# Weight conversion in 4 KB pieces that also lie in w2's own tile, with three, then five ticks a slot

## The chip, the cores and the metric

The kernel runs on one core of one Trainium2 chip. The metric is the device time of one execution in microseconds (us). Three timed runs of the kernel before gave 1628.86, 1624.64 and 1628.58 us; the median is 1628.58 us.

## The reference

Eight batches of threshold attention (8 heads, 576 positions, 64 features a head) feed a block of layer norm and two matrix products:

```python
scores = scale * np.matmul(q, k.transpose(0, 1, 3, 2))
thresh = np.max(scores, axis=-1, keepdims=True) - tau
scores = np.where(scores >= thresh, scores, -1000000000.0)
attn = np.exp(scores - np.max(scores, axis=-1, keepdims=True))
attn = attn / (np.sum(attn, axis=-1, keepdims=True) + 1e-09)
x = (attn @ v, heads side by side)            # (8, 576, 512)
xn = (x - mu) / np.sqrt(var + 1e-06) * g_ln
out = x + np.maximum(xn @ w_ch1, 0.0) @ w_ch2  # 512 -> 2048 -> 512
```

The two weight matrices arrive as 64-bit floats. [...]

## The kernel before, in words

**Slots.** The attention of one batch is cut into nine slots (s = 0 to 8), 72 slots in all (n = 0 to 71). One slot is: score products on TensorE (`scores`, L324, or L100 for s = 4), row maxima on VectorE (L337), exponentials on ScalarE (L348), threshold and row sums on VectorE (`weights`, L354, then the reciprocal L358), and four multiplications by that reciprocal. Then the weights are transposed: in batch 0 on TensorE (L384, L397, with copies on ScalarE), from batch 1 on by VectorE (L415, L421) and a round trip through DRAM (L427 out, L436 and L437 back). One slot later they are multiplied by v (L460) and the result is copied to x (L477, on ScalarE). Scores and values share PSUM, so the next slot's scores wait for this copy.

**Feed-forward.** Every 288 tokens form a group. A group needs 64 products with w1 (xc to hidden) and 64 with w2 (hidden to p), each two matmuls by `product` (L100). They fill TensorE's idle time inside the slots: `second_part` issues as many steps in each of four quarters of a slot as keep the group on schedule, about 29 a slot. A step whose weights are not yet converted, by the plan's own count, is not issued (`yield 0`, L545, L572); TensorE catches up in later slots.

**Conversion.** The weights are 32 chunks of 128x512 numbers, 16 of w1 and 16 of w2. The class `Weights` moves them along by ticks, at most one of each per tick: `begin` (two operations on VectorE, L211 and L215, two on ScalarE, L219 and L220), `carry` (an integer addition on GpSimd, L226) and, three ticks later, `end` (a selection on VectorE, L231; for w1 a multiplication by g on ScalarE, L236, which writes w1). `fetch` issues the DMA of a chunk's 512 KB (L199). A chunk in work occupies one place of 8 KB per partition: 4 KB of raw words, 2 KB for `a`, 2 KB for `y`. There are five such places: two in `stage`, two in `hidden` (until chunk 10), one in `et`'s buffer (until chunk 24). A place is given back by `end`, which issues the next fetch into it at once. Ticks are at points 0 and 2 of slots 0 to 3, at 0, 2 and 3 of slots 4 and 5, and at 0 to 3 from slot 6 on (L649).

**Order.** Every engine runs its instructions in the order in which this Python code writes them; nothing is reordered. SyncE (SP) issues nearly all DMAs in one queue, and an instruction that waits there holds back all behind it.

Of the kernel before, what the change touches and what calls it, by code (L numbers as in the profile page):

```python
# [18 lines left out]
def kernel(  # L19
# [66 lines left out]
    w2_sb = [consts.tile([128, DM], F32, name=f"w2_{i}") for i in range(ND)]  # L86
# [73 lines left out]
    class Weights:  # L160
# [12 lines left out]
        def __init__(self):  # L173
            self.chunks = [
                (w1_sb[i][:, c : c + WC], w_ch1[i * 128 : (i + 1) * 128, c : c + WC], i)
                for c in range(0, DF, WC)
                for i in range(NK)
            ] + [(w2_sb[i], w_ch2[i * 128 : (i + 1) * 128, :], None) for i in range(ND)]
            self.n1 = NK * (DF // WC)
            self.fetched = self.begun = self.carried = self.ended = 0  # L180
            self.at, self.due, self.ticks = {}, [], 0
            flat = hidden.rearrange("p d t -> p (d t)")
            stage = consts.tile([128, 2 * 4 * WC], F32, name="stage")
            et0 = att.tile([128, NB, 128], F32, tag="et", bufs=1, name="et0")
            own = [stage[:, i * 4 * WC : (i + 1) * 4 * WC] for i in range(2)]
# [15 lines left out]
        def parts(self, i):
            at = self.at[i][0]
            raw = at[:, : 2 * WC]
            both = lambda t: raw.bitcast(t).rearrange("p (n two) -> p n two", two=2)
            return both, at[:, 2 * WC : 3 * WC], at[:, 3 * WC :]

        def begin(self):
            both, a, y = self.parts(self.begun)
            self.begun += 1
            au, hi = a.bitcast(U32), both(U32)[:, :, 1]  # L210
# [8 lines left out]
            nc.scalar.activation(both(I32)[:, :, 0], both(U32)[:, :, 0], func=AF.Copy, scale=2.0**-29)  # L219
            nc.scalar.activation(y, both(F32)[:, :, 1], func=AF.Square)  # L220

        def carry(self):
            both, a, y = self.parts(self.carried)
            self.carried += 1
            ai = a.bitcast(I32)
            nc.gpsimd.tensor_tensor(out=ai, in0=ai, in1=both(I32)[:, :, 0], op=ALU.add)  # L226

        def end(self):
            both, a, y = self.parts(self.ended)
            dst, _, gi = self.chunks[self.ended]  # L230
# [403 lines left out]
    if w_ch1.dtype == I64:  # L634
        conversion.fetch()
    else:
# [10 lines left out]
    for n in range(NS):  # L647
        b, s = divmod(n, SLOTS)
        ticks = ((0, 2) if n < 4 else (0, 2, 3) if n < 6 else (0, 1, 2, 3))  # L649
# [10 lines left out]
        run(n, 0)  # L660
        run_all(stores)
# [10 lines left out]
        weights(b, es, thr)  # L672
# [64 lines left out]
```

## Time and profile before

| | |
|---|---|
| median of three runs | 1628.58 us |
| profiled execution, its own time | 1629.46 us |
| its span in the trace | 1627.6 us |
| TensorE busy | 1438.3 us, 88% |
| VectorE busy | 832.7 us, 51% |
| ScalarE busy | 463.3 us, 28% |
| GpSimd busy | 456.1 us, 28% |
| granted TensorE clock, mean | 0.957 |

Busy shares are means over the whole span. The span has two parts: about 400 us in which weights are converted and the first groups run, and a regular part in which every nine slots look alike. A share of the span says little about the first part, so it is read slot by slot. A slot is taken to begin with its first row maximum (L337).

### The profile page before, as it was taken

The numbers are of one execution on the slowest core, as the hardware profiler recorded it, in microseconds if no ns is written. First come the engines' busy times: TensorE is split into PE (matmuls) and PEld (weight loads), VectorE is DVE, ScalarE is ACT, GpSimd is POOL, SyncE is SP. The second block draws the span as 40 slices with busy tenths as digits, with TensorE's granted clock in tenths as the row PEclk, the third lists the DMA queues.
The fourth block names the chain that finished last, engine by engine and source line by source line (L and its number), as shares of the span: only waits on it lengthen the run. The fifth ranks groups of instructions, "written<-read, shape, count | busy, mean of one in ns | idle before, by whom it ended". The sixth has DMA issues, their size and how long they took to land.

```text
span 1627.6 us, 28865 instructions
## 1 busy us (share of the span) xinstructions
PE 1438.3 (88%) x11700; PEld 851.4 (52%) x11700; DVE 832.7 (51%) x1380; ACT 463.3 (28%) x831; POOL 456.1 (28%) x703
## 2 busy tenths in 40 slices
PE   3658834899989999999999999899999999999998
PEld 2434412565555655555555655565555655555554
DVE  6767655324455554655555554645555554645210
ACT  4666522122313231232313131322223131323120
POOL 3444332212222222323232332323132322323100
PEclk9778957999999999999999999999999999999999
DMA  8322345533567455755566446655566547645400
GB/s 160 98 69 82 78 114 136 142 85 79 120 151 175 125 141 124 162 150 141 133 149 171 128 128 146 151 152 128 146 143 164 128 128 165 149 122 138 111 11 15
DMA packets 460694, 205.08 MB, mean 126 GB/s; under 512 B 275024, under 2 KB 420176, under 8 KB 460560
## 3 DMA queue, kind: packets, MB, share of 16 engines
q1 hardware_dynamic: 458160, 202.93, 51.0%
q8 instruction: 92, 1.51, 0.4%
q10 hardware_dynamic: 2368, 0.30, 0.1%
q14 instruction: 42, 0.34, 0.1%
q0 software_dynamic: 32, 0.00, 0.0%
HBM read 119.41 MB, written 83.76 MB: 125 GB/s over the span
## 4 chain that ended last, share of the span: by engine, by line
PE 60%; SPq 10%; DVE 10%; issue 6%; ACT 5%; DMA 5%; POOL 3%; POOLq 0%; DVEq 0%; ACTq 0%
PE p L100 42%; PE sc L460 8%; PE sc L324 7%; SPq L112 7%; DVE e L354 3%; DMA em<-scr 3%; DVE neg L337 2%; ACT e L348 2%; SPq L427 2%; POOL e L363 2%; PE sc L100 2%; DVE et L421 1%; ACT hidden L554 1%; PE tp L384 1%; DMA stage<-in_moe_w_ch_dram 1%
## 5 line engine op out<-in xcount | busy, mean ns | idle before, releaser
L100 PE MATMUL p<-hidden,w 128*64 128x288 f32 x4096 | 518.4, 409 | 46.6 <-DVE w L231 46.6
L100 PE MATMUL p<-xc,w 128*64 128x288 f32 x4096 | 523.4, 411 | 30.9 <-ACT hidden L554 25.5
L100 PEld LDWEIGHTS p<-hidden,w 128*64 128x64 f32 x4096 | 298.1, 138 | 240.9 <-DVE w L231 49.3
L100 PEld LDWEIGHTS p<-xc,w 128*64 128x64 f32 x4096 | 293.5, 138 | 240.5 <-ACT hidden L554 45.3
L337 DVE TENSOR_REDUCE neg<-sc 128x2 f32<-128x1152 f32 x144 | 189.6, 1353 | 347.2 <-PE sc L324 269.8
L363 POOL TENSOR_SCALAR e<-e,den 128x576 f32<-128x576 f32 x270 | 207.4, 785 | 359.7 <-DVE den L358 330.2
L348 ACT ACTIVATE e<-sc,neg 128x576 f32<-128x576 f32 x288 | 194.1, 743 | 269.6 <-DVE neg L337 269.4
L354 DVE SCALAR_TENSOR_TENSOR e<-sc,thr,e 128x576 f32<-128x576 f32 x288 | 220.0, 813 | 37.1 <-ACT e L348 36.4
L324 PE MATMUL sc<-kT,qT 64*128 64x512 f32 (+3 forms) x1024 | 159.8, 452 | 36.4 <-DVE e L354 10.8
L421 DVE STREAM_TRANSPOSE et<-e 128x1152 f32<-128x1152 f32 x112 | 152.8, 1371 | 67.8 <-POOL e L363 60.4
L460 PE MATMUL sc<-em,v_in 128*64 128x256 f32 (+1 forms) x1536 | 158.3, 353 | 26.4 <-DMA em<-scr 17.9
L554 ACT ACTIVATE hidden<-p 128x288 f32<-128x288 f32 x256 | 103.2, 413 | 267.5 <-PE p L100 267.4
L324 PEld LDWEIGHTS sc<-kT,qT 64*128 64x128 f32 x1024 | 88.9, 197 | 122.7 <-issue 78.0
L341 POOL TENSOR_SCALAR thr<-neg,low_sb 128x2 f32<-128x2 f32 x144 | 38.9, 270 | 373.5 <-DVE neg L337 373.5
L460 PEld LDWEIGHTS sc<-em,v_in 128*64 128x64 f32 x1536 | 102.8, 147 | 77.1 <-issue 28.7
L477 ACT COPY x<-sc 128x256 f32<-128x256 f32 x64 | 23.7, 371 | 361.7 <-PE sc L460 346.0
L518 DVE TENSOR_TENSOR o<-p,rb 128x288 f32<-128x288 f32 x64 | 28.1, 439 | 124.9 <-PE p L100 124.9
L519 POOL TENSOR_TENSOR o<-o,x 128x288 f32<-128x288 f32 x64 | 50.9, 796 | 111.7 <-DVE o L518 111.2
L486 POOL TENSOR_TENSOR sum<-sum,x 128x256 f32<-128x256 f32 (+1 forms) x64 | 32.7, 511 | 143.8 <-ACT x L477 141.2
L269 DVE STREAM_TRANSPOSE kT<-k_in 128x576 f32<-128x576 f32 x32 | 24.8, 775 | 90.2 <-DMA k_in<-in_k_dram 86.3
L460 PE MATMUL sc<-rest,v_rest 128*64 128x256 f32 (+1 forms) x384 | 50.9, 340 | 0.0
L566 DVE RECIPROCAL rb<-rb 128x288 f32<-128x288 f32 x16 | 31.3, 1954 | 37.8 <-ACT rb L565 37.8
(71 smaller groups left out, 684.4 us busy)
## 6 DMA issues: line engine op xcount, KB each, us to landing
scr<-et SPq DMA_DIRECT2D x252, 288.0 KB, 4.9
em<-scr SPq DMA_DIRECT2D x63, 1024.0 KB, 5.9
stage<-in_moe_w_ch_dram SPq DMA_DIRECT2D x22, 512.0 KB, 3.9
q_in<-in_q_dram SPq DMA_DIRECT2D x128, 72.0 KB, 3.3
out_dram<-ot SPq DMA_DIRECT2D x256, 36.0 KB, 4.2
k_in<-in_k_dram SPq DMA_DIRECT2D x124, 72.0 KB, 2.6
v_in<-in_v_dram SPq DMA_DIRECT2D x64, 128.0 KB, 2.6
rest<-scr SPq DMA_DIRECT2D x63, 128.0 KB, 5.9
```

The costliest lines, as they stand in the source:

```text
L100: nc.tensor.matmul(out[r], lhsT=lhsT[:, r], rhs=rhs, **flags)
L112: (engines[i] if engines else nc.sync).dma_start(out=t[32 * g : 32 * g + 32], in_=src[b, 2 * hp + h, :, 32 * e : 32 * e + 32].rearrange("( ...
L324: nc.tensor.matmul(sc[h][:, at : at + n], lhsT=qT[r, half, j * 128 : (j + 1) * 128], rhs=kT[r, o : o + n], start=True, stop=True,)
L337: nc.vector.tensor_reduce(out=neg[:, i], in_=sc[h][:, : 2 * S].rearrange("p (j n) -> p j n", j=2), axis=AXL.X, op=ALU.max, negate=True,)
L341: nc.gpsimd.tensor_scalar(out=thr[:, i], in0=neg[:, i], scalar1=-1.0, scalar2=low_sb, op0=ALU.mult, op1=ALU.add,)
L348: nc.scalar.activation(es[:, i], blocks[i], func=AF.Exp, bias=neg[:, i : i + 1])
L354: nc.vector.scalar_tensor_tensor(out=es[:, i], in0=blocks[i], scalar=thr[:, i : i + 1], in1=es[:, i], op0=ALU.is_ge, op1=ALU.mult, accum_o ...
L363: nc.gpsimd.tensor_scalar(out=es[:, i], in0=es[:, i], scalar1=den[:, i : i + 1], scalar2=1.0, op0=ALU.mult, op1=ALU.mult,)
L421: nc.vector.transpose(et[:, :, 64 * h : 64 * h + 64].rearrange("p n (j c) -> p j n c", j=2), es[:, 2 * h : 2 * h + 2].rearrange("p j (n c) ...
L460: nc.tensor.matmul(dst[64 * h : 64 * h + 64], lhsT=vt[:, c, h, :] if c < J else vr[:, h, :], rhs=pick(em[:, c] if c < J else er, hp, h), s ...
L519: nc.gpsimd.tensor_tensor(out=o, in0=o, in1=groups[g][:, m], op=ALU.add)
L554: nc.scalar.activation(hidden[:, d], p1, func=AF.Relu)
```

## The change: what it does

1. **Pieces.** A place of 8 KB becomes two pieces of 4 KB: one holds the raw words from the fetch to the `carry`, the other holds `a` and `y` from `begin` to `end`. `w2` is now one tile, and its 64 KB per partition are used as eight pieces until the chunks that belong there are made. Four pieces lie in `hidden`, two in `et`'s buffer, four in `stage`.
2. **Fetches** are no longer issued by `end`, but at two points of a slot (after `run(n, 0)` and before `run(n, 3)`), at most two at a time, and only into pieces freed two or more ticks ago. Five are issued at the start.
3. **A piece for `a` and `y`** may be one that was given back in the same tick, by `end` or by `carry`.
4. **Ticks** are at points 0, 2 and 3 of slots 0 to 5, and at 0 to 4 from slot 6 on.
5. **GpSimd** multiplies w1's chunks by g (ScalarE before, L236), and in batch 0 all four parts of the attention weights by the reciprocal (before, ScalarE did two, L361).

```diff
-            self.free = [(at, len(self.chunks)) for at in own]
-            self.free += [(flat[:, i * 4 * WC : (i + 1) * 4 * WC], 10) for i in range(2)]
-            self.free.append((et0.rearrange("p n c -> p (n c)")[:, : 4 * WC], 24))
+            for t, n, before in (
+                (w2_sb, ND // 2, lambda p: n1 + 2 * p),
+                (hidden, 4, lambda p: 10),
+                (et, 2, lambda p: 2 * n1),
+                (stage, 4, lambda p: 2 * n1),
+            ):
+                for p in range(n):
+                    self.free.append((before(p), -1, flat(t)[:, p * 2 * WC : (p + 1) * 2 * WC]))
+        def piece(self, i, wait):
+            fit = [p for p in self.free if p[0] > i and p[1] < self.ticks - wait]
...
+            got = min(fit, key=lambda p: p[0])
+        def fetch(self, most=99):
+            while self.fetched < len(self.chunks) and most:
+                i = self.fetched
+                if sum(p[0] > i for p in self.free) <= 2:
+                    break
+                got = self.piece(i, 1)
...
         def begin(self):
-            both, a, y = self.parts(self.begun)
+            i = self.begun
+            got = self.piece(i, -1)
...
         def carry(self):
...
+            self.give(self.raw.pop(i))
         def end(self):
...
             if gi is not None:
-                nc.scalar.mul(dst, a, g_sb[:, gi : gi + 1])
-            self.free.append(self.at.pop(self.ended))
-            self.ended += 1
-            self.fetch()
+                nc.gpsimd.tensor_scalar(
+                    out=dst, in0=a, scalar1=g_sb[:, gi : gi + 1], scalar2=1.0,
+                    op0=ALU.mult, op1=ALU.mult,
+                )
+            self.give(got)
...
         for i in range(4):
-            if b == 0 and i >= 2:
-                nc.scalar.mul(es[:, i], es[:, i], den[:, i : i + 1])
-                continue
             nc.gpsimd.tensor_scalar(
...
-        ticks = ((0, 2) if n < 4 else (0, 2, 3) if n < 6 else (0, 1, 2, 3))
+        ticks = (0, 2, 3) if n < 6 else range(5)
...
         run(n, 0)
+        conversion.fetch(2)
         run_all(stores)
...
+        run_all(aside)
+        conversion.fetch(2)
         run(n, 3)
```

The order in which the engines now meet their work is shown at three places.

VectorE in slot 1, from the reciprocal to the next row maximum, before:

```order
L358 RECIPROCAL den<-den 128x4 [waits DVE_49]
L231 SCALAR_TENSOR_TENSOR stage<-stage 128x512
L211 TENSOR_SCALAR hidden<-hidden 128x512
L215 SCALAR_TENSOR_TENSOR hidden<-hidden 128x512 [waits DVE_49]
L231 SCALAR_TENSOR_TENSOR stage<-stage 128x512
L211 TENSOR_SCALAR et_157<-et_157 128x512
L215 SCALAR_TENSOR_TENSOR et_157<-et_157 128x512 [waits DVE_49]
L337 TENSOR_REDUCE neg<-sc_154 128x2 [waits PE_49,Activation_49]
```

and now (L393 is the reciprocal, L266 `end`'s selection, L239 and L243 are `begin`, L372 the row maximum; w_89 is w2's tile, Pool is GpSimd):

```order
L393 RECIPROCAL den<-den 128x4 [waits DVE_49]
L266 SCALAR_TENSOR_TENSOR hidden<-hidden 128x512
L239 TENSOR_SCALAR hidden<-w_89 128x512 [waits Pool_49]
L243 SCALAR_TENSOR_TENSOR hidden<-w_89,hidden 128x512 [waits DVE_49]
L266 SCALAR_TENSOR_TENSOR hidden<-hidden 128x512
L239 TENSOR_SCALAR hidden<-w_89 128x512 [waits Pool_49]
L243 SCALAR_TENSOR_TENSOR hidden<-w_89,hidden 128x512 [waits DVE_49]
L266 SCALAR_TENSOR_TENSOR hidden<-hidden 128x512
L239 TENSOR_SCALAR hidden<-w_89 128x512 [waits Pool_49]
L243 SCALAR_TENSOR_TENSOR hidden<-w_89,hidden 128x512 [waits DVE_49]
L372 TENSOR_REDUCE neg<-sc_139 128x2 [waits PE_49,Activation_49]
```

Three chunks stand where two stood, and each `begin` now waits for GpSimd, since its piece was given back in the same tick.

GpSimd in the same slot, from the first multiplication by the reciprocal to the next threshold, before:

```order
L363 TENSOR_SCALAR e<-e,den 128x576 [waits DVE_49]
L363 TENSOR_SCALAR e<-e,den 128x576
L226 TENSOR_TENSOR hidden<-hidden 128x512 [waits Activation_49]
L226 TENSOR_TENSOR hidden<-hidden 128x512 [waits DVE_49,Activation_49]
L341 TENSOR_SCALAR thr<-neg,low_sb 128x2 [waits DVE_49] x2
```

and now (L395 is the multiplication by the reciprocal, L271 that by g, L257 the addition, L376 the threshold):

```order
L395 TENSOR_SCALAR e<-e,den 128x576 [waits DVE_49]
L395 TENSOR_SCALAR e<-e,den 128x576 x3
L271 TENSOR_SCALAR w_1_86<-hidden,g_sb 128x512 [waits DVE_49]
L257 TENSOR_TENSOR hidden<-hidden 128x512 [waits Activation_49,Pool_49]
L271 TENSOR_SCALAR w_2_87<-hidden,g_sb 128x512 [waits DVE_49]
L257 TENSOR_TENSOR hidden<-hidden,w_89 128x512 [waits Activation_49]
L271 TENSOR_SCALAR w_3_88<-hidden,g_sb 128x512 [waits DVE_49]
L257 TENSOR_TENSOR hidden<-hidden,w_89 128x512 [waits DMAHW6_49,Activation_49,Pool_49]
L376 TENSOR_SCALAR thr<-neg,low_sb 128x2 [waits DVE_49] x2
```

Four multiplications stand ahead of the first conversion work instead of two, and three multiplications by g and one more addition are added.

TensorE in slot 9, from the last weight transposes of batch 0 to the next scores, before (x counts matmuls, two a product):

```order
L384 MATMUL tp<-ident,e 128x128 x16
L397 MATMUL tr<-ident,e 64x128 x4
L100 MATMUL p_1258<-hidden,w_7_96 64x288 x2
L100 MATMUL p_1258<-hidden,w_8_97 64x288 x2
L460 MATMUL sc_154<-em,v_in 64x256 x8
L460 MATMUL sc_154<-rest_109,v_rest_114 64x256 x2
L100 MATMUL p_1258<-hidden,w_9_98 64x288 x2
L324 MATMUL sc_154<-kT,qT 128x512
```

and now:

```order
L416 MATMUL tp<-ident,e 128x128 x16
L429 MATMUL tr<-ident,e 64x128 x4
L100 MATMUL p_1290<-hidden,w_89 64x288 x18
L100 MATMUL p_1429<-hidden,w_89 64x288 x18
L492 MATMUL sc_139<-em,v_in 64x256 x8
L492 MATMUL sc_139<-rest_94,v_rest_99 64x256 x2
L100 MATMUL p_1429<-hidden,w_89 64x288 x12
L359 MATMUL sc_139<-kT,qT 128x512
```

Three products with w2 were issued in this slot, now 24. Counted the same way, slots 9 to 15 hold 3, 2, 3, 32, 38, 71 and 51 products before (200), and 24, 33, 29, 27, 29, 29 and 29 now (200); all other slots are unchanged within one product.

SyncE from slot 9 on, before:

```order
L436 DMA em<-scr 128x4x512
L437 DMA rest_109<-scr 64x512
L199 DMA stage<-in_moe_w_ch_dram 128x512 x2
L427 DMA scr<-et 32x18x128 x4
L112 DMA q_in<-in_q_dram 32x18x32 x4
L112 DMA k_in<-in_k_dram 32x18x32 x4
L126 DMA v_in<-in_v_dram 128x4x64
```

and now:

```order
L468 DMA em<-scr 128x4x512
L469 DMA rest_94<-scr 64x512
L563 DMA out_dram<-ot 32x9x32 x8
L459 DMA scr<-et 32x18x128 x4
L112 DMA q_in<-in_q_dram 32x18x32 x4
L112 DMA k_in<-in_k_dram 32x18x32 x4
L126 DMA v_in<-in_v_dram 128x4x64
```

The last six weight fetches stood behind the first round trips of the attention weights; now the last fetch is issued in slot 8, ahead of all of them. The last chunk was ended in slot 11, now it is in slot 9; by the start of slot 9, 24 chunks were ended, now 31.

## Rows read from the trace of the kernel before

**Rows 1.** Part 2 of the page: TensorE's busy tenths in 40 slices.

```profile
PE   3658834899989999999999999899999999999998
```

**Rows 2.** Busy time by stretch: slots 0–5, 6–8, 9–15, 18–24, 36–42.

```profile
core 0: us, PE busy (x) PEld busy (x) DVE busy (x) ACT busy (x) POOL busy (x), PEclk, DMA share, GB/s
14.02:115.61 101.59, 58.02 (x373) 36.59 (x374) 74.25 (x122) 61.84 (x107) 47.03 (x50) 0.82 0.40 97
115.61:196.58 80.97, 66.37 (x462) 38.40 (x463) 51.34 (x78) 46.41 (x82) 29.74 (x29) 0.88 0.33 86
196.58:401.15 204.57, 146.37 (x1162) 84.32 (x1163) 89.79 (x151) 44.47 (x77) 53.51 (x76) 0.85 0.42 105
441.35:584.19 142.84, 135.22 (x1142) 82.30 (x1142) 76.19 (x130) 33.41 (x60) 41.52 (x69) 0.99 0.60 146
805.08:945.79 140.71, 134.68 (x1142) 79.19 (x1142) 76.11 (x131) 33.41 (x60) 41.54 (x69) 0.99 0.61 148
```

**Rows 3.** Waits in 197 to 305 us: total, times, longest.

```profile
PE p L100 <- DVE w L231: 46.6, 5, 19.6
ACT stage L219 <- DMA stage<-in_moe_w_ch_dram: 31.8, 3, 15.8
DVE stage L211 <- DMA stage<-in_moe_w_ch_dram: 21.0, 2, 14.7
```

**Rows 4.** Timeline of VectorE in slot 10: start, length, in brackets its idle time.

```profile
226.39 0.78 DVE L269 STREAM_TRANSPOSE kT<-k_in 128x576 f32<-128x576 f32 x1 [7.99 <-DMA k_in<-in_k_dram]
...
235.17 0.43 DVE L211 TENSOR_SCALAR stage<-stage 128x512 uint32<-128x512 uint32 x1 [6.27 <-DMA stage<-in_moe_w_ch_dram]
...
261.59 0.43 DVE L211 TENSOR_SCALAR stage<-stage 128x512 uint32<-128x512 uint32 x1 [14.71 <-DMA stage<-in_moe_w_ch_dram]
```

**Rows 5.** Waits of SyncE's DMA queue in 0 to 300 us.

```profile
SPq L199 <- POOL stage L226: 72.8, 15, 12.9
SPq L427 <- DVE et L421: 45.4, 3, 17.6
```

**Rows 6.** Stretches from reciprocal's end to next row maximum, slots 0 to 5.

```profile
26.41:29.64 3.23, 3.23 (x15) 2.31 (x14) 2.79 (x5) 3.20 (x6) 3.13 (x3) 1.00 0.78 138
37.87:43.77 5.90, 4.54 (x32) 2.74 (x29) 4.98 (x7) 5.17 (x9) 5.85 (x4) 0.90 0.72 146
51.92:59.87 7.95, 7.40 (x33) 4.00 (x30) 5.05 (x7) 5.17 (x9) 6.74 (x5) 0.52 0.67 172
67.71:75.43 7.72, 4.22 (x18) 1.88 (x20) 5.02 (x6) 5.17 (x9) 6.71 (x5) 0.63 0.21 67
85.89:95.67 9.78, 4.53 (x17) 2.47 (x18) 9.26 (x10) 7.00 (x12) 8.62 (x6) 0.72 0.17 54
104.14:115.61 11.47, 4.46 (x17) 2.40 (x18) 6.31 (x10) 7.15 (x13) 8.29 (x11) 0.64 0.28 91
```

**Rows 7.** Timeline of slot 3 behind its reciprocal, all engines.

```profile
67.53 0.18 DVE L358 RECIPROCAL den<-den 128x4 f32<-128x4 f32 x1
67.62 0.66 DVE L231 SCALAR_TENSOR_TENSOR et<-et 128x512 f32<-128x512 f32 x1
...
70.81 0.34 ACT L477 COPY x<-sc 128x256 f32<-128x256 f32 x1
...
71.21 6.74 PE L100 MATMUL sc<-kT,q_diag 128*64 128x512 f32 x32 [4.24 <-ACT x L477]
...
75.43 1.36 DVE L337 TENSOR_REDUCE neg<-sc 128x2 f32<-128x1152 f32 x1 [2.63 <-PE sc L100]
```

**Rows 8.** Single lines by tile: count, shortest/median/longest in ns.

```profile
L363 POOL TENSOR_SCALAR e<-e,den x270: 733/745/1691, 26.5 to 1520.4; 128x576 f32<-128x576 f32 x135
...
L226 POOL TENSOR_TENSOR stage<-stage x22: 1273/1290/1742, 28.7 to 275.9; 128x512 int32<-128x512 int32 x22
...
L215 DVE SCALAR_TENSOR_TENSOR stage<-stage x22: 691/1068/1672, 12.0 to 268.7; 128x512 uint32<-128x512 uint32 x22
```

**Rows 9.** Groups of GpSimd's instructions in 14 to 116 us: busy, mean ns, idle.

```profile
L363 POOL TENSOR_SCALAR e<-e,den 128x576 f32<-128x576 f32 x12 | 15.8, 1320 | 32.6 <-DVE den L358 32.6
```

**Rows 10.** Timeline of VectorE at the start of slot 6.

```profile
123.05 0.43 DVE L211 TENSOR_SCALAR et<-et 128x512 uint32<-128x512 uint32 x1 [4.22 <-ACT w L236]
```

More of the change, by code (lines that the diff above doesn't have):

```diff
@@ L85 @@
     w1_sb = [consts.tile([128, DF], F32, name=f"w1_{i}") for i in range(NK)]
-    w2_sb = [consts.tile([128, DM], F32, name=f"w2_{i}") for i in range(ND)]
+    w2_sb = consts.tile([128, ND, DM], F32, name="w2")
     q_diag = [consts.tile([128, 128], F32, name=f"q_diag{i}") for i in range(HP)]
@@ L177, in __init__ @@
                 for i in range(NK)
-            ] + [(w2_sb[i], w_ch2[i * 128 : (i + 1) * 128, :], None) for i in range(ND)]
+            ] + [(w2_sb[:, i], w_ch2[i * 128 : (i + 1) * 128, :], None) for i in range(ND)]
             self.n1 = NK * (DF // WC)
             self.fetched = self.begun = self.carried = self.ended = 0
-            self.at, self.due, self.ticks = {}, [], 0
-            flat = hidden.rearrange("p d t -> p (d t)")
-            stage = consts.tile([128, 2 * 4 * WC], F32, name="stage")
@@ L201, in parts @@
[L201 to L205, printed above, removed]
-        def begin(self):
-            both, a, y = self.parts(self.begun)
+            self.raw, self.made, self.due, self.ticks = {}, {}, [], 2
+            flat = lambda t: t.rearrange("p a b -> p (a b)")
+            stage = consts.tile([128, 8, WC], F32, name="stage")
@@ new lines, in piece @@
+        def piece(self, i, wait):
+            fit = [p for p in self.free if p[0] > i and p[1] < self.ticks - wait]
+            if not fit:
+                return None
+            got = min(fit, key=lambda p: p[0])
+            self.free = [p for p in self.free if p is not got]
+            return got
+        def fetch(self, most=99):
[4 more added lines that the diff above has]
+                got = self.piece(i, 1)
+                if got is None:
+                    break
+                most -= 1
+                self.fetched += 1
+                self.raw[i] = got
+                nc.sync.dma_start(out=got[2].bitcast(I64), in_=self.chunks[i][1])
@@ L209, in begin, with give, words @@
+        def give(self, got):
+            self.free.append((got[0], self.ticks, got[2]))
+        def words(self, i, t):
+            return self.raw[i][2].bitcast(t).rearrange("p (n two) -> p n two", two=2)
+        def begin(self):
+            i = self.begun
+            got = self.piece(i, -1)
+            if got is None:
+                return
+            self.made[i] = got
+            a, y = got[2][:, :WC], got[2][:, WC:]
             self.begun += 1
-            au, hi = a.bitcast(U32), both(U32)[:, :, 1]
+            self.due.append(self.ticks + 3)
+            au, hi = a.bitcast(U32), self.words(i, U32)[:, :, 1]
@@ L218, in begin @@
             )
[L219 to L220 removed]
+            nc.scalar.activation(
+                self.words(i, I32)[:, :, 0], self.words(i, U32)[:, :, 0],
+                func=AF.Copy, scale=2.0**-29,
+            )
+            nc.scalar.activation(y, self.words(i, F32)[:, :, 1], func=AF.Square)
         def carry(self):
[L223 removed]
+            i = self.carried
             self.carried += 1
[L225 to L226 removed]
+            ai = self.made[i][2][:, :WC].bitcast(I32)
+            nc.gpsimd.tensor_tensor(out=ai, in0=ai, in1=self.words(i, I32)[:, :, 0], op=ALU.add)
+            self.give(self.raw.pop(i))
         def end(self):
[L229 to L230 removed]
+            i = self.ended
+            self.ended += 1
+            got = self.made.pop(i)
+            a, y = got[2][:, :WC], got[2][:, WC:]
+            dst, _, gi = self.chunks[i]
             nc.vector.scalar_tensor_tensor(
@@ L634 @@
     if w_ch1.dtype == I64:
-        conversion.fetch()
+        conversion.fetch(5)
     else:
@@ L671 @@
         second_part(n, 1)
[L672 removed]
+        weights(es, thr)
         run_all(aside)
```

21 lines of the change are left out of this document (7 added, 14 removed).

## The prediction

> **What bounds the kernel now.** I first read the page's slices [rows 1]. A slice is 40.7 us. From slice 9 on TensorE is busy nine tenths nearly throughout. In the first eight it is not, and slices 6 and 7 (the digits 3 and 4, about 203 to 285 us) are a hole that comes after slices in which TensorE was already at 8. A change to the weight conversion acts ahead of the regular part alone, so I cut that part into stretches by slots [rows 2].
>
> Slots 9 to 15 take 204.57 us. They hold 200 feed-forward products. Slots 18 to 24 are the same seven places of a later batch, also with 200 products, and take 142.84 us; one batch earlier or later it is much the same (140.71 us for slots 36 to 42). TensorE is busy 146.37 us of the 204.57 and 135.22 of the 142.84. So slots 9 to 15 cost 61.7 us more than the regular part, nearly all of it TensorE standing still: 58.2 us idle against 7.6.
>
> What it stands still for is in the waits of 197 to 305 us [rows 3]: products wait 46.6 us in five waits for VectorE's selection L231, that is for a chunk of w2. VectorE in turn waits 21.0 us and ScalarE 31.8 us for the DMA of a chunk. In slot 10 VectorE stands 6.27 us and then 14.71 us in front of L211 for raw words that have not landed, and earlier 7.99 us for k [rows 4]. SyncE says why they land late [rows 5]: its fetches waited 72.8 us, in fifteen waits, for GpSimd to be done with the old place (a fetch is issued by the `end` that frees it), and behind these stand k, q and the round trips, whose own wait for `et` is 45.4 us. One late chunk therefore holds up the attention too. In the plan it leaves 3, 2 and 3 products in slots 9 to 11, and 71 and 51 to catch up with in slots 14 and 15.
>
> **The change, part by part.**
>
> *The hole.* With twice as many pieces and earlier ticks, 31 of 32 chunks are ended by the start of slot 9, and the plan issues 24 to 33 products in each of slots 9 to 15. No fetch is behind a round trip any more. What is late next is TensorE itself, as in slots 18 to 24. I take their 142.84 us plus 2 us for the one chunk still left in slot 9 and the first loads of batch 1: 204.57 − 144.8 = 59.8 us gained. The bounds: at most 204.57 − 140.71 = 63.9; at least, if only the products' wait for L231 goes and the lateness of k and the round trips stays, about 40 of the 46.6 us.
>
> *What the early slots pay.* Slots 0 to 3 get a third chunk each, and in slots 0 to 5 the work behind the reciprocal changes its shape. Here a slot is a chain: row maximum, exponentials, reciprocal, then conversion work on VectorE while ScalarE copies x, scores run, and the next row maximum comes. In slot 3 the copy comes 3.1 us after the reciprocal, scores follow, and the row maximum starts 7.7 us after it, released by TensorE [rows 7]. From the reciprocal to the next row maximum slots 0 to 5 take 3.23, 5.90, 7.95, 7.72, 9.78 and 11.47 us, 46.1 in sum [rows 6]; nothing in front of the reciprocal is changed.
>
> Now GpSimd comes first: four multiplications M instead of two, 0.745 us each alone and 1.32 us in this stretch beside VectorE [rows 8, 9]. Behind them stand an addition A, 1.29 us [rows 8], and a multiplication by g, G, on 512 columns: by M's rows 0.66 us (0.745 × 512/576) to 1.17. `begin` (B: L211 and L215, 0.43 + 0.69 = 1.1 us alone [rows 8, 10], up to 2.5 beside GpSimd) waits for the A or G that frees its piece, and the next A waits for B. The two engines take turns, which costs waits but keeps durations near the short end; I take M 0.8, A 1.35, G 0.75, B 1.3 to 1.7, a selection 0.66 [rows 7].
>
> Slot 0 in full: 4M 3.2, A 1.35, B 1.3, A 1.35, B 1.3, selection 0.66, G 0.75, A 1.35, B 1.3 make 12.6 us instead of 3.23; scores are long done. Slot 1: 4M 3.2, G 0.75, B 1.6, selection and B 2.3 twice with a short wait for G and A, about 11.5 instead of 5.90. Slot 2 has one old piece and so waits for GpSimd only once: 10 instead of 7.95. Slot 3 has two old pieces, but its third waits for the addition of the same tick, behind 4M at 1.3, two G, three A and the sum: 13.3 instead of 7.72. Slot 4: 4M, then three times G, B and selection: 12.4 instead of 9.78. Slot 5: the copy of x waits in ScalarE's queue for an addition, the sums over x for the copy, and the third `begin` for an addition behind these: about 16.5 instead of 11.47. The sum is 76.3, so 30 us are lost. The bounds: if all handovers were hidden, only the added VectorE work of four chunks counts, 4 × 1.8 = 7 us; if M, G and B all ran at their long values, a slot would cost some 4 us more, 54 us in all.
>
> *Slots 6 to 8* get five ticks instead of four, 2.3 us of VectorE and 1.35 of GpSimd more a slot, and no G, since from chunk 16 on w2 is written. TensorE is busy 66.37 of 80.97 us there [rows 2], and between reciprocal and row maximum the products hide VectorE. ScalarE is rid of two multiplications and of L236, for which VectorE waited 4.22 us at the start of slot 6 [rows 10]. I take zero, between −5 and +15.
>
> One rule speaks against the move to GpSimd. The measured rows come first: M takes 0.745 us alone and 1.32 us on the mean in 14 to 116 us [rows 8, 9], and L215 goes from 0.69 to 1.67 us. The Trainium skill (GPSIMD Engine Reference, Engine selection and Key points) says that elementwise work belongs on VectorE, GpSimd being about half as fast with two inputs and about equal with one, and that the two share SBUF interfaces, with contention when VectorE has two inputs or a two-port mode. The rows agree on the contention; by that rule every B beside an M is slow, which is the upper bound of 54 us above and the third rival, not the sum.
>
> **The sum.** −59.8 + 30 + 0 is about −30 us. The profiled execution took 1629.46 us (span 1627.6), so 1599.7; the median of the runs is 0.9 us lower. I write 1599.
>
> **The rivals.**
>
> *The conversion hides in the early slots.* For it: ScalarE loses its two multiplications by the reciprocal and those by g there, and TensorE idles 43.6 of 101.59 us [rows 2]. Against it: the row maximum stands behind `begin` in VectorE's own queue, so a wait there cannot be hidden. It would cost 7 to 12 us, and the time would be 1629 − 60 + 10 = 1579.
>
> *The hole closes by half.* k, q and the round trips may be late for reasons of their own; `et` alone held SyncE 45.4 us [rows 5]. Against it: in slots 18 to 24 the same DMAs run without such a hole at more traffic (146 GB/s against 105 [rows 2]). Gain 40, cost 30 to 35: 1622.
>
> *Slower: GpSimd becomes the bound of slots 0 to 8.* The place is the queue behind the reciprocal: four M, then A and G, for which VectorE's next `begin` and so the next row maximum wait. With the long durations slots 0 to 5 lose 54 us, and slots 6 to 8, where five additions and four M then stand in the way of four ticks behind the reciprocal, 5 to 7 us each. That is 72 against 60: 1641. It decides from a loss of 6.6 us a slot over nine slots. Against it: VectorE is idle while it waits for GpSimd, and then M runs at 0.745.
>
> **How the numbers follow.** Forecast 0.65 (its own range 1588 to 1612), hidden 0.15, half a hole 0.12, slower 0.08. The range 1578 to 1620 holds the forecast, nearly all of the first rival, and the better part of the second. The measurement of this kernel tells 0.3%, 5 us, from no change. Faster by that: the forecast, the first rival and most of the second, 0.87; within it: the rest of the second and the edge between, 0.05; slower 0.08.
>
> **What would show it.** Right: slots 9 to 15 take 140 to 150 us, and no wait of TensorE for L266 is over 2 us; from reciprocal to row maximum slots 0 to 5 take 70 to 85 us, with VectorE waiting for GpSimd in front of L239, about 12 us in slot 0 alone; slots 6 to 8 within 76 to 96 us; from slot 16 on nothing moves. Wrong: L239 still waits for DMAs, or the chain of the first 100 us shows no GpSimd in front of `begin`, or slots 9 to 11 still wait for k.

## The result, and the profile after

The changed kernel takes 1591.21 us (median of four runs, 1588.33 to 1592.15), the kernel before, beside it, 1628.72 (1624.64 to 1631.95). The ratio is 0.9768, with a 95% interval of 0.9742 to 0.9794. The forecast was 1599. The profiled execution took 1588.33 us, its span is 1586.6.

TensorE's 40 slices of the profile after (39.7 us each now) answer to [rows 1]:

```profile
PE   3556789999989998999989998999989999999998
```

The digits 3 and 4 of slices 6 and 7 are now 8 and 9; those of slices 2 to 5 went from 6, 5, 8, 8 to 5, 5, 6, 7. The stretches by slots, which answer to [rows 2], come first for slots 0–5, 6–8 and 9–15, then for all that follows (columns as there):

```profile
14.07:143.37 129.30, 65.69 (x376) 42.66 (x377) 82.55 (x133) 52.20 (x91) 67.78 (x82) 0.67 0.44 116
143.37:222.85 79.48, 63.21 (x460) 37.74 (x459) 57.41 (x85) 42.78 (x76) 41.28 (x38) 0.89 0.21 55
222.85:364.98 142.13, 137.47 (x1162) 83.26 (x1163) 77.29 (x132) 36.23 (x65) 41.91 (x69) 0.99 0.56 133
364.98:1586.60 1221.62, 1160.97 (x9692) 688.79 (x9690) 614.43 (x1020) 308.05 (x562) 321.74 (x530) 0.99 0.55 134
```

The same last stretch in the kernel before:

```profile
401.15:1627.60 1226.45, 1163.11 (x9692) 689.83 (x9690) 613.64 (x1020) 308.08 (x562) 321.36 (x530) 0.99 0.55 134
```

| slots | before | after | difference | forecast |
|---|---|---|---|---|
| 0–5 | 101.59 | 129.30 | +27.7 | +30 |
| 6–8 | 80.97 | 79.48 | −1.5 | 0 |
| 9–15 | 204.57 | 142.13 | −62.4 | −59.8 |
| 16 to the end | 1226.45 | 1221.62 | −4.8 | 0 |

The stretches from the reciprocal's end to the next row maximum, slots 0 to 5, answer to [rows 6]:

```profile
25.97:37.84 11.87, 6.16 (x23) 4.21 (x22) 3.88 (x9) 3.57 (x7) 7.35 (x8) 0.50 1.00 244
46.01:57.37 11.36, 7.64 (x34) 4.50 (x32) 7.79 (x10) 3.45 (x6) 8.89 (x10) 0.65 0.86 237
65.54:76.97 11.43, 6.65 (x42) 4.19 (x38) 8.65 (x10) 3.26 (x6) 11.26 (x11) 0.80 0.80 236
85.07:98.17 13.10, 5.94 (x46) 2.81 (x42) 6.68 (x10) 2.41 (x6) 11.82 (x11) 0.89 0.25 81
106.28:120.19 13.91, 6.44 (x29) 3.70 (x24) 8.68 (x10) 3.87 (x7) 9.84 (x11) 0.63 0.24 75
128.30:143.37 15.07, 5.08 (x20) 3.03 (x21) 6.17 (x9) 3.48 (x7) 10.84 (x16) 0.67 0.00 0
```

They sum to 76.7 us (46.1 before). VectorE is busy 41.87 us of them and waits in the rest. Its timeline in slot 0 shows for whom (start, length, operation; in brackets the idle time before it):

```profile
25.79 0.18 DVE L393 RECIPROCAL den<-den 128x4 f32<-128x4 f32 x1
30.25 0.43 DVE L239 TENSOR_SCALAR hidden<-hidden 128x512 uint32<-128x512 uint32 x1 [4.28 <-POOL w L257]
...
32.95 0.43 DVE L239 TENSOR_SCALAR hidden<-hidden 128x512 uint32<-128x512 uint32 x1 [1.54 <-POOL hidden L257]
...
36.77 0.43 DVE L239 TENSOR_SCALAR hidden<-hidden 128x512 uint32<-128x512 uint32 x1 [2.06 <-POOL hidden L257]
```

The same 12 us on GpSimd:

```profile
26.08 2.90 POOL L395 TENSOR_SCALAR e<-e,den 128x576 f32<-128x576 f32 x4 [6.33 <-DVE den L393]
28.94 1.27 POOL L257 TENSOR_TENSOR w<-w,hidden 128x512 int32<-128x512 int32 x1
31.64 1.28 POOL L257 TENSOR_TENSOR hidden<-hidden 128x512 int32<-128x512 int32 x1 [1.42 <-ACT hidden L247]
34.80 0.69 POOL L271 TENSOR_SCALAR w<-w,g_sb 128x512 f32<-128x512 f32 x1 [1.89 <-DVE w L266]
35.46 1.27 POOL L257 TENSOR_TENSOR hidden<-hidden 128x512 int32<-128x512 int32 x1
```

Read side by side, the engines take turns: each `begin` (L239) starts when the addition that frees its piece has ended, and the first of them stands behind four multiplications. The waits of VectorE in 14 to 144 us add this up (total, times, longest):

```profile
DVE w L239 <- POOL w L257: 9.1, 3, 3.8
DVE w L239 <- POOL w L271: 8.6, 4, 3.5
...
DVE hidden L239 <- POOL w L271: 6.1, 2, 3.5
DVE hidden L239 <- POOL w L257: 4.3, 1, 4.3
...
DVE hidden L239 <- POOL hidden L257: 3.6, 2, 2.1
```

That is 31.7 us, in twelve waits. In 210 to 305 us, by contrast, the list of VectorE's waits holds no DMA of raw words (the 64-bit weights as they arrive) any more, where [rows 3] have 21.0 us, and in 222 to 305 us TensorE's has no wait for `end`, where they have 46.6; k is waited for 2.4 us in sum.

### The profile page after: what moved, and what is told of

Same layout as the page of the kernel before. It is cut to its first block, busy times and chain, and to the rows that moved or that the text cites. A ratio compares the mean times of both kernels' runs of the same rounds, so it can differ in the third digit from the quotient of the medians.

```text
span 1586.6 us, 28851 instructions
## 1 busy us (share of the span) xinstructions
PE 1431.7 (90%) x11700; PEld 854.8 (54%) x11700; DVE 835.3 (53%) x1380; ACT 441.8 (28%) x797; POOL 477.1 (30%) x737
## 4 chain that ended last, share of the span: by engine, by line
PE 64%; DVE 8%; SPq 8%; DMA 6%; issue 5%; ACT 4%; POOL 4%; POOLq 0%; ACTq 0%; DVEq 0%
PE p L100 45%; PE sc L492 9%; PE sc L359 7%; SPq L112 5%; DMA em<-scr 4%; DVE neg L372 3%; ACT e L383 3%; POOL e L395 2%; DVE e L389 2%; PE sc L100 2%; SPq L459 2%; ACT hidden L586 1%; SPq L126 1%; SPq L130 1%; DVE et L453 1%
## 5 line engine op out<-in xcount | busy, mean ns | idle before, releaser
L100 PE MATMUL p<-xc,w 128*64 128x288 f32 x4096 | 521.2, 409 | 26.3 <-ACT hidden L586 24.2
L100 PE MATMUL p<-hidden,w 128*64 128x288 f32 x4096 | 515.7, 408 | 0.0
L100 PEld LDWEIGHTS p<-xc,w 128*64 128x64 f32 x4096 | 293.5, 137 | 232.7 <-ACT hidden L586 43.8
L100 PEld LDWEIGHTS p<-hidden,w 128*64 128x64 f32 x4096 | 298.8, 138 | 192.5 <-issue 2.7
L372 DVE TENSOR_REDUCE neg<-sc 128x2 f32<-128x1152 f32 x144 | 189.4, 1353 | 315.3 <-PE sc L359 252.4
L395 POOL TENSOR_SCALAR e<-e,den 128x576 f32<-128x576 f32 x288 | 219.4, 779 | 332.8 <-DVE den L393 300.8
L492 PE MATMUL sc<-em,v_in 128*64 128x256 f32 (+1 forms) x1536 | 154.1, 347 | 16.4 <-DMA em<-scr 11.3
L359 PEld LDWEIGHTS sc<-kT,qT 64*128 64x128 f32 x1024 | 89.4, 198 | 128.3 <-issue 79.5
L376 POOL TENSOR_SCALAR thr<-neg,low_sb 128x2 f32<-128x2 f32 x144 | 39.2, 272 | 363.9 <-DVE neg L372 362.9
L416 PE MATMUL tp<-ident,e 128*128 128x128 f32 x144 | 26.7, 334 | 28.9 <-ACT em L423 28.5
```

The source lines that it names most:

```text
L100: nc.tensor.matmul(out[r], lhsT=lhsT[:, r], rhs=rhs, **flags)
L359: nc.tensor.matmul(sc[h][:, at : at + n], lhsT=qT[r, half, j * 128 : (j + 1) * 128], rhs=kT[r, o : o + n], start=True, stop=True,)
L372: nc.vector.tensor_reduce(out=neg[:, i], in_=sc[h][:, : 2 * S].rearrange("p (j n) -> p j n", j=2), axis=AXL.X, op=ALU.max, negate=True,)
L376: nc.gpsimd.tensor_scalar(out=thr[:, i], in0=neg[:, i], scalar1=-1.0, scalar2=low_sb, op0=ALU.mult, op1=ALU.add,)
L395: nc.gpsimd.tensor_scalar(out=es[:, i], in0=es[:, i], scalar1=den[:, i : i + 1], scalar2=1.0, op0=ALU.mult, op1=ALU.mult,)
L492: nc.tensor.matmul(dst[64 * h : 64 * h + 64], lhsT=vt[:, c, h, :] if c < J else vr[:, h, :], rhs=pick(em[:, c] if c < J else er, hp, h), s ...
```

## The experiments

Each was timed beside the kernel before on its chip, whose medians there were 1626.43 (first four runs), 1632.96 (next four), 1627.42 (next three) and 1630.69 (last). What a run says is read mostly from its stretches: from slot 16 on, where all have almost the same work, the profiled executions lie between 1219.5 and 1231.5 us, so a few microseconds of a total settle nothing.

**1. The changed kernel with the ticks of before.** Fetch rule and GpSimd's work stay, and the pieces but for `et`'s two, which end at chunk 24.

```diff
-                (et, 2, lambda p: 2 * n1),
+                (et, 2, lambda p: 24),
-        ticks = (0, 2, 3) if n < 6 else range(5)
+        ticks = ((0, 2) if n < 4 else (0, 2, 3) if n < 6 else (0, 1, 2, 3))
```

> The changed kernel with the ticks of the kernel before (0, 2; from slot 4 0, 2, 3; from slot 6 0 to 3), and et's two pieces only for chunks below 24, as before. By the plan 24 chunks are ended at the start of slot 9 and slots 9 to 12 hold 4, 2, 2 and 8 products, fewer than before. Theory (the hole cost 62 us because fetches waited in SyncE's queue in front of k, q and the round trips; a thin slot by itself costs only the idle time of a chain of 15 to 18 us): slots 9 to 12 take 62 to 75 us together instead of 108.8, slots 0 to 3 lose less than with three ticks, the time is 1598 to 1612. Rival (the ticks alone close the hole): 1622 or more. Rival (ticks do not matter): 1594 or less.

Measured: 1647.65 us, ratio 1.0136 (1.012 to 1.0151). The theory failed; the time is the first rival's. Slots 9–15 take 211.07 us, more than before the change, and slots 9–11 alone 89.4. VectorE's timeline there:

```profile
238.86 0.43 DVE L239 TENSOR_SCALAR w<-stage 128x512 uint32<-128x512 uint32 x1 [14.04 <-DMA stage<-in_moe_w_ch_dram]
...
268.51 0.43 DVE L239 TENSOR_SCALAR stage<-stage 128x512 uint32<-128x512 uint32 x1 [12.56 <-DMA stage<-in_moe_w_ch_dram]
```

The next slot has one more such wait (14.76 us). SyncE's queue in the same run shows why:

```profile
224.27 3.88 SPq L459 DMA_DIRECT2D scr<-et  x4
228.25 4.10 SPq L112 DMA_DIRECT2D q_in<-in_q_dram  x4
232.39 2.12 SPq L112 DMA_DIRECT2D k_in<-in_k_dram  x4
234.61 0.92 SPq L221 DMA_DIRECT2D stage<-in_moe_w_ch_dram  x2
...
264.29 0.44 SPq L221 DMA_DIRECT2D stage<-in_moe_w_ch_dram  x1
```

A ring: the fetch stands behind the store of the weights and 6 us of issuing q and k; the store waits for VectorE's transposes; these stand behind a `begin` that waits for the fetch. Once round is one slot, so one or two chunks a slot come through, however many pieces are free.

**2. The kernel before with a third tick in slots 0 to 3**, and nothing else.

```diff
-        ticks = ((0, 2) if n < 4 else (0, 2, 3) if n < 6 else (0, 1, 2, 3))
+        ticks = (0, 2, 3) if n < 6 else (0, 1, 2, 3)
```

> The kernel before with one part of the change alone: ticks 0, 2 and 3 in slots 0 to 5 (0 to 3 from slot 6 on, as before). By the plan 26 chunks instead of 24 are ended at the start of slot 9, and slots 9 and 10 hold 5 and 3 products. Theory (places of 8 KB and fetches at the selection keep SyncE waiting): the hole is one slot shorter, slots 0 to 3 pay some 8 us, the time is 1608 to 1628. Rival (earlier ticks are what gains): 1604 or less.

Measured: 1611.76 us, 0.9911 (0.9894 to 0.9928), as the theory had it. Slots 0–5 take 113.92 us, 12.3 more than before; slots 9–15 178.14, 26.4 less. So in the old places the third tick costs less than half of what slots 0–5 pay in the changed kernel, and it alone takes 26.4 of the 62.4 us out of slots 9–15.

**3. `begin` takes the piece that has been free longest**, not the one that is lost first.

```diff
-            got = min(fit, key=lambda p: p[0])
+            got = min(fit, key=(lambda p: p[0]) if wait > 0 else (lambda p: (p[1], p[0])))
```

> The changed kernel, but begin takes the piece that has been free longest instead of the one with the nearest deadline, so no begin waits for GpSimd in its own tick. Theory (the 28 us lost in slots 0 to 5 are VectorE waiting 31.7 us for GpSimd in front of begin): slots 0 to 5 take 106 to 117 us instead of 129.3, the time is 1570 to 1579. Rival (they are the third chunk's own work and GpSimd's longer queue, which the selection waits for too): slots 0 to 5 stay at 124 or more, the time is 1585 to 1595.

Measured: 1578.46 us, 0.9708 (0.9693 to 0.9722). Slots 0–5 take 114.97 us, 14.3 less than in the changed kernel. The list of VectorE's waits has none in front of L239 any more, but of the 31.7 us of waits only those 14.3 show in the slots. One part of the rest turned up one instruction later, in front of the selection (VectorE in 14 to 135 us):

```profile
DVE w L266 <- POOL w L257: 5.2, 2, 2.6
DVE stage L266 <- POOL stage L257: 5.1, 2, 2.6
DVE et L266 <- POOL et L257: 2.6, 1, 2.6
DVE hidden L266 <- POOL hidden L257: 2.6, 1, 2.6
```

Another went into durations. In the changed kernel the multiplications by the reciprocal take 926 ns on the mean in slots 0–5:

```profile
L395 POOL TENSOR_SCALAR e<-e,den 128x576 f32<-128x576 f32 x24 | 21.9, 926 | 31.4 <-DVE den L393 20.8 <-PE sc L492 10.6
```

and in this run, where VectorE works beside them, 1222:

```profile
L395 POOL TENSOR_SCALAR e<-e,den 128x576 f32<-128x576 f32 x24 | 29.0, 1222 | 31.5 <-DVE den L393 20.9 <-PE sc L492 10.7
```

**4. ScalarE does two of the four multiplications by the reciprocal again**, in batch 0.

```diff
+            if b == 0 and i >= 2:
+                nc.scalar.mul(es[:, i], es[:, i], den[:, i : i + 1])
+                continue
```

> The changed kernel, but in batch 0 ScalarE again does two of the four multiplications by the reciprocal. Theory: GpSimd's queue in front of the first addition is 1.5 us shorter in each of nine slots, part of it given back by ScalarE: 1579 to 1588. Rival (GpSimd's length is the whole price): 1560 to 1577. Rival (no part of the price): 1589 to 1595.

Measured: 1582.65 us, 0.9734 (0.9719 to 0.9748). Slots 0–5 take 120.28 us, 9.0 less than in the changed kernel. So in the changed kernel this move to GpSimd was a loss there.

**5. Both edits, 3 and 4.**

> Both single edits that gained apart: begin takes the piece that has been free longest (alone 1578.5), and ScalarE again does two of the four multiplications by the reciprocal in batch 0 (alone 1582.7). Theory (both shorten the same wait of VectorE for GpSimd behind the reciprocal, so they do not add up; what is left in slots 0 to 5 is the third tick, 113.9 us in the kernel before with three ticks): slots 0 to 5 take 109 to 115 us, the time is 1572 to 1579. Rival (they add up): 1566 to 1571.

Measured: 1570.86 us (1567.56 to 1572.05), 0.9625 (0.958 to 0.9671): the interval lies wholly below that of the changed kernel, and this version beats both kernels. Slots 0–5 take 104.32 us, 25.0 less than in the changed kernel, while the edits alone saved 14.3 and 9.0. They add up, as the rival said. The third tick's 12.3 us were no floor either: slots 0–5 pay 2.7 us over the kernel before. With an old piece and two multiplications off GpSimd, `begin` runs beside GpSimd (VectorE in slot 2, behind its reciprocal):

```profile
59.10 0.42 DVE L239 TENSOR_SCALAR hidden<-w 128x512 uint32<-128x512 uint32 x1
59.56 1.03 DVE L243 SCALAR_TENSOR_TENSOR hidden<-w,hidden 128x512 uint32<-128x512 uint32 x1
...
64.28 0.69 DVE L266 SCALAR_TENSOR_TENSOR stage<-stage 128x512 f32<-128x512 f32 x1 [1.18 <-POOL stage L257]
64.88 0.85 DVE L239 TENSOR_SCALAR hidden<-hidden 128x512 uint32<-128x512 uint32 x1
65.77 1.66 DVE L243 SCALAR_TENSOR_TENSOR hidden<-hidden 128x512 uint32<-128x512 uint32 x1
```

One short wait is left. Several operations are slower here than in slot 0 of the changed kernel (L243 1.03 and 1.66 us against 0.69), but VectorE hardly stands still.

**6 and 7. g on ScalarE again**, in the changed kernel (6) and with edits 3 and 4 (7).

```diff
-                nc.gpsimd.tensor_scalar(
-                    out=dst, in0=a, scalar1=g_sb[:, gi : gi + 1], scalar2=1.0,
-                    op0=ALU.mult, op1=ALU.mult,
-                )
+                nc.scalar.mul(dst, a, g_sb[:, gi : gi + 1])
```

> The changed kernel with the multiplication by g on ScalarE again, all else as changed. Theory (the wait of begin for a piece given back in the same tick costs slots 0 to 5 31.7 us, 14.7 of it for the multiplication by g behind GpSimd's four multiplications): those 14.7 us shrink to the 4 to 8 that ScalarE's own queue takes, so 1580 to 1588. Rival (ScalarE then copies x later, scores and row maxima follow later, which eats the gain): 1590 to 1600, with the row maximum waiting for TensorE in slots 0 to 5.

> The same two edits, and the multiplication by g on ScalarE again, so that GpSimd has none of the moved work. Theory (with a piece that has long been free begin waits for no engine, so where g is done changes little; ScalarE's longer queue delays the copy of x by some 0.7 us in slots 0 to 5): within 4 us of the run with the two edits alone. Rival (GpSimd's queue still sets the slots, since 15.5 us of waits for its additions are left in front of the selection in the run with old pieces alone): 5 to 10 us faster than that run.

Measured for 6: 1589.14 us, 0.9737 (0.9679 to 0.9794). Slots 0–5 take 120.49 us, 8.8 less; but slots 6–8 are 2.4 longer, slots 9–15 2.9, the rest 3.0. The total cannot be told from the changed kernel's, so on the time neither side won. On the stretch the theory did: `begin` waits 4.0 us for the multiplication by g, where 14.7 were and 4 to 8 were expected. Measured for 7: 1574.05 us, 0.9649 (0.9605 to 0.9693), 3.2 us above run 5, as the theory had it. Slots 0–5 take 109.49 us, 5.2 more than in run 5. So moving g to GpSimd cost 8.8 us there as long as `begin` waited for it, and saved 5.2 once `begin` did not.

**8. Fetches from `end` again**, into any free piece.

```diff
-                got = self.piece(i, 1)
+                got = self.piece(i, -1)
...
             self.give(got)
+            self.fetch()
...
-        conversion.fetch(2)
```

> The changed kernel with its fetch rule undone: each end issues a fetch again, into any piece that is free, the one just given back too; the two points of a slot and the age of two ticks are gone. Pieces, ticks and the moves to GpSimd stay. In the order 31 chunks are ended by the start of slot 9 as in the changed kernel, and slots 9 to 12 hold 28, 29, 29 and 28 products. Theory (what closes the hole is that the ticks end the chunks before slot 9, the fetch rule is worth little): slots 9 to 15 take 140 to 147 us, the time is 1585 to 1600. Rival (the fetch rule keeps SyncE clear of GpSimd's additions, and without it k, q and raw words come late in slots 0 to 8): 1606 or more, with VectorE waiting for DMAs in front of L239 or the transposes of k.

Measured: 1600.55 us, 0.9807 (0.976 to 0.9855), half a microsecond past the theory's upper end. Slots 0–5 take 128.64 us, 6–8 84.08 (4.6 more than in the changed kernel), 9–15 146.14 (4.0 more). The medians differ by 9.3 us, but the intervals of the two ratios overlap, so what the fetch rule is worth is not settled. It is not what closes the hole: slots 9–15 stay within 4.0 us.

**9 and 10. Which ticks?** Run 5 with four ticks from slot 6 on (9), and with two ticks in slots 0 to 3 (10); in both, the pieces of `et` end at chunk 24.

```diff
-        ticks = (0, 2, 3) if n < 6 else range(5)
+        ticks = (0, 2, 3) if n < 6 else range(4)                              # 9
+        ticks = (0, 2) if n < 4 else (0, 2, 3) if n < 6 else range(5)         # 10
```

> The run with old pieces and split multiplications (1570.9), with four ticks a slot from slot 6 on instead of five, the early third tick kept; the two pieces in the buffer of et are used only up to chunk 24, as before the change. In the order 27 chunks are ended by the start of slot 9 (30 in that run), two fetches are left for slots 9 and 10, and slots 9 to 12 hold 5, 2, 1 and 32 products. Theory (all or nothing: as long as one fetch stands behind the round trips of slot 9, every later chunk comes a slot later, however many are ended): slots 9 to 15 take 190 to 211 us, the time is 1610 to 1637. Rival (a share: the hole of 61.7 us goes by the chunks that are late, 31 - 24 = 7, so some 9 us for each of the three): 1590 to 1604.

> The other half: old pieces and split multiplications with five ticks from slot 6 on, but two ticks in slots 0 to 3 as before the change; pieces of et up to chunk 24. 26 chunks are ended by the start of slot 9, and slots 9 to 12 hold 5, 2, 9 and 32 products. Theory (all or nothing): slots 0 to 5 take 90 to 100 us, slots 9 to 15 take 180 to 205, the time is 1605 to 1630. Rival (a share, four chunks late at 9 us, less 4 to 10 us for the early slots): 1592 to 1603.

Measured: 1612.54 us, 0.9918 (0.9884 to 0.9952), and 1614.74 us, 0.9916 (0.9886 to 0.9946). Slots 9–15 take 192.16 and 198.86 us. With 27 and 26 of 32 chunks ended by slot 9 that is 47.1 and 53.8 us more than in run 5 (145.09), where a share would be 27 and 36. So both came as the theory had it. But both took `et`'s two pieces back for the last eight chunks together with the tick, so they do not tell ticks from pieces. Nor is it strictly all or nothing: run 2, also with 26 ended, has 178.14 us. One thing that differs is how many products the plan can issue in slots 9–11: 5, 3 and 32 in run 2, but 5, 2 and 1 in run 9 and 5, 2 and 9 in run 10.

**11. Three of the four multiplications on ScalarE**, from run 5 (`i >= 1` in place of `i >= 2`).

> The run with old pieces and split multiplications, with three of the four multiplications by the reciprocal on ScalarE in batch 0 instead of two. Theory (what is left of the wait of the selection for GpSimd's additions, 7.2 us in slots 0 to 5, goes; ScalarE's copy of x moves back by one multiplication and the scores with it, which the conversion on VectorE mostly covers): 1564 to 1572. Rival (the chain over ScalarE takes over: its mult stands in front of the copy of x): 1574 to 1582, with the row maxima of slots 0 to 5 waiting for TensorE.

Measured: 1569.65 us, 0.9656 (0.9621 to 0.969), the same as run 5. The wait for GpSimd is gone, as the theory had it, but row maxima now wait for scores, as the rival had it (VectorE in 14 to 119 us):

```profile
DVE neg L372 <- PE sc L359: 4.9, 4, 1.6
```

Two more such waits, of L100, take 1.9 us. Slots 0–5 are 4.3 us longer (108.60); the total does not show it. No gain.

**12. Fetches from ScalarE's queue**, in run 10, to cut the ring.

```diff
-                nc.sync.dma_start(out=got[2].bitcast(I64), in_=self.chunks[i][1])
+                nc.scalar.dma_start(out=got[2].bitcast(I64), in_=self.chunks[i][1])
```

> The kernel with two ticks in slots 0 to 3 and five from slot 6 on (1614.7), with its weight fetches issued from ScalarE's queue instead of SyncE's, in the same places of the program; nothing else is changed, so slots 9 to 12 still hold 5, 2, 9 and 32 products. Theory (the hole is a ring through SyncE's queue: the fetch stands behind the store of the weights and the loads of q and k, the store waits for VectorE's transposes, and these stand behind a begin that waits for the fetch of the slot before): VectorE's 28.4 us of waits for raw words in 185 to 300 us fall under 10, slots 9 to 15 take 150 to 178 us instead of 198.9, the time is 1566 to 1594. Rival (the pieces come free late, and the thin plan of slots 9 to 11 costs by itself): slots 9 to 15 stay above 185 us, the time is 1602 or more.

Measured: 1607.79 us, 0.9852 (0.983 to 0.9875). The ring is cut. VectorE's wait for raw words in 185 to 305 us falls from

```profile
DVE stage L239 <- DMA stage<-in_moe_w_ch_dram: 28.4, 4, 15.1
```

in run 10, whose list has no wait for k, to this in run 12, with one for k in its place:

```profile
DVE kT L304 <- DMA k_in<-in_k_dram: 14.3, 2, 8.7
...
DVE stage L239 <- DMA stage<-in_moe_w_ch_dram: 3.5, 1, 3.5
```

Slots 9–15 only fall from 198.86 to 184.43 us: between the two expectations, and the time is the rival's. (Slots 0–5 take 99.57 us, 4.2 more than in run 10.) Split into slots 9–11 and 12–15, run 10 reads:

```profile
190.49:276.70 86.21, 34.12 (x198) 18.32 (x199) 43.29 (x73) 16.65 (x28) 23.41 (x29) 0.64 0.45 113
276.70:389.35 112.65, 110.79 (x966) 67.30 (x966) 43.30 (x71) 24.95 (x45) 26.86 (x45) 1.00 0.41 99
```

run 12:

```profile
197.17:268.95 71.78, 34.97 (x198) 18.73 (x199) 43.10 (x73) 16.28 (x28) 23.60 (x29) 0.67 0.56 137
268.95:381.60 112.65, 110.79 (x966) 67.33 (x966) 43.31 (x72) 24.98 (x45) 26.95 (x45) 1.00 0.40 98
```

the kernel before:

```profile
196.58:278.37 81.79, 30.19 (x164) 15.03 (x163) 46.66 (x79) 19.40 (x32) 25.84 (x30) 0.65 0.44 113
278.37:401.15 122.78, 116.18 (x998) 69.29 (x1000) 43.13 (x74) 25.06 (x45) 27.67 (x46) 0.99 0.41 100
```

and the changed kernel:

```profile
222.85:287.58 64.73, 60.84 (x478) 35.28 (x479) 36.48 (x67) 15.44 (x28) 19.75 (x30) 0.97 0.55 122
287.58:364.98 77.40, 76.64 (x686) 47.99 (x686) 40.81 (x65) 20.80 (x37) 22.16 (x39) 1.00 0.56 141
```

Less waiting for DMAs shortens the first line (86.21 to 71.78) and leaves the second as it is to a hundredth. The second is TensorE at work (110.79 of 112.65 us): the products that the plan did not issue in slots 9–11 because their chunk was not ended yet. Slots 12–15 hold 184 products in runs 10 and 12 (200 less 16), 192 before, 114 after. Runs 10 and 12 have the same plan, so what slots 12–15 cost follows the plan and not the waits.

What a slot saves when it lacks its products is seen in the kernel before, by its row maxima (slot 9 begins at 196.58, [rows 2]):

```profile
215.78 2.62 DVE L337 TENSOR_REDUCE neg<-sc 128x2 f32<-128x1152 f32 x2 [1.54 <-PE sc L324]
...
262.66 2.61 DVE L337 TENSOR_REDUCE neg<-sc 128x2 f32<-128x1152 f32 x2
...
278.37 2.61 DVE L337 TENSOR_REDUCE neg<-sc 128x2 f32<-128x1152 f32 x2
```

A regular slot takes 20.4 us (142.84 / 7). Slot 11, with 3 products and no wait of VectorE for a DMA, takes 15.7, slot 9 19.2, and slot 10, which holds the waits for k and for raw words of [rows 4], 46.9. So a thin slot without such a wait saves up to 4.7 us, while the 26 or so products that it puts off cost some 13 us later, at 0.51 us each ((116.18 − 76.64) / 78).

## Why the prediction was right, and where its reasons were not

*The hole: −59.8 forecast, −62.4 measured.* The size was right because it was read off a whole stretch that runs the same work later, slots 18–24, and not summed from waits. The reading that it was "nearly all of it TensorE standing still" holds as well: TensorE's idle time in slots 9–15 fell from 58.2 to 4.7 us, and the same 1162 matmuls took 8.9 us less (137.47 against 146.37), at a mean granted clock of 0.99 of full speed against 0.85. The lower bound, "about 40 of the 46.6 us", was kept, but it took the wait for L231 for the loss, and most of the time did not come off where that wait was. By the lines above, only 17.1 of the 62.4 us lie in slots 9–11, where the waits of [rows 3] are. The other 45.4 lie in slots 12–15 (122.78 − 77.40), where TensorE is hardly ever idle: 39.5 us of them are its additional work there (116.18 − 76.64), 78 products put off at 0.51 us. Against regular slots, slot 10 was 26.5 us longer, slots 9 and 11 together 5.9 shorter, slots 12–15 41.2 longer.

*What closes it.* The prediction named "twice as many pieces and earlier ticks" and did not part them. (Of the pieces, w2's tile has 32 KB per partition, eight times 4 KB, and not 64 KB.) Pieces, fetch rule and moves without the new ticks gain nothing (run 1, 1647.65). The third tick alone, in the old places, gains 26.4 of the 62.4 us (run 2). With the fifth tick or the early third one taken back, and `et`'s pieces for the last eight chunks with it, 47.1 and 53.8 us are lost again (runs 9 and 10). So the ticks are needed; whether all of them are, and what the pieces add, stays open. How open can be counted, without a run, in the order that the Python code gives: with run 9's four ticks and `et`'s pieces up to chunk 29 instead of 24, slots 9 to 12 would hold 6, 51, 29 and 28 products instead of 5, 2, 1 and 32; with all the new ticks in the kernel before and its places of 8 KB, 7, 50, 29 and 28.

*The early slots: +30 forecast, +27.7 measured.* From reciprocal to row maximum 76.3 was forecast and 76.7 came. Slot by slot, forecast to measured: 12.6 to 11.9, 11.5 to 11.4, 10 to 11.4, 13.3 to 13.1, 12.4 to 13.9, 16.5 to 15.1. Misses of up to 1.5 us cancel. In slot 2 one `begin` waited, as forecast (2.67 us), but the selection behind it took 1.76 us instead of 0.66. The statement that nothing in front of the reciprocal is changed was off by 3.0 us in sum (55.54 us before, 52.56 after), mostly in slot 4, where that part went from 10.5 to 8.1 us. The mechanism was as described, twelve waits of `begin` for a piece given back in the same tick, 31.7 us. The runs give the causes sizes that depend on each other. The third tick costs 12.3 us in the kernel before (run 2), 18.4 in the changed kernel (129.30 − 110.88, run 1) and 9.0 in run 5 (104.32 − 95.35, run 10). `begin`'s choice of piece costs 14.3, the two more multiplications on GpSimd 9.0. Without both, and with two ticks in slots 0 to 3, slots 0–5 are 6.2 us shorter than in the kernel before (run 10).

*Slots 6–8*, 0 forecast, −1.5 measured, within the bounds. *From slot 16 on*, 0 forecast, −4.8 measured: TensorE's busy time is 2.1 us shorter and the work the same, and the runs with the same plan there spread over more than that. The cause of these 4.8 us stays open.

*The sum.* −62.4 + 27.7 − 1.5 − 4.8 is −41.0 us by the profiled executions; the medians give −37.5. The forecast's −30 misses by small terms of one sign in every row of the table.

*The rivals.* Hiding in the early slots did not happen (27.7 us against 7 to 12). Closing by half did not: k is waited for 2.4 us. GpSimd as the bound: its place was right, its price was not. The multiplications took 926 ns on the mean, nearer to the 0.8 us taken than to 1.32, with VectorE waiting beside them; in run 3, where it works, they go to 1222. In these runs the long durations and the waits did not come together, and the 54 us needed both.

## What to carry to other kernels

When a resource is late for a few slots, count what the plan puts off because of it, and not only the waits: here the waits were in slots 9–11, but 45.4 of the 62.4 us came off in slots 12–15, where TensorE was busy with what had been put off. A buffer pool with a free piece should hand out the one released longest ago, since the piece just released carries a wait into the queue of whoever takes it, and that wait can decide whether moving other work to another engine gains or loses. A fetch that shares an in-order queue with the transfers it delays should be through before they begin; moving it to another queue (run 12) cut the waits for raw words from 28.4 to 3.5 us, but 14.3 us of waits for k came in their place.

## What the hardware showed that was not expected

Side by side, GpSimd and VectorE lost in durations a part of what they saved in waits. The multiplication by the reciprocal took 0.73 us each while VectorE stood still (2.90 us for four in slot 0), 1.22 on the mean with old pieces, and 1421 ns in run 5 (14 to 119 us), where VectorE hardly waits:

```profile
L398 POOL TENSOR_SCALAR e<-e,den 128x576 f32<-128x576 f32 x12 | 17.0, 1421 | 31.4 <-DVE den L393 31.4
```

VectorE's L243 went from 0.69 to 1.66 us in the same way. In spite of both, run 5 takes 25.0 us less than the changed kernel in slots 0–5.
